# Attention and two mixers on one core: places in a hand-written order of steps, and which PSUM bank a sum reads first

## The chip, the cores and the metric

One core of a Trainium2 chip runs the whole program. The metric is the device time of one execution in microseconds (us), here the median of several runs. TensorE (PE) multiplies, VectorE (DVE) and ScalarE (ACT) do elementwise work, GpSimd (POOL) a few integer additions, SyncE (SP) only issues DMAs.

## What is computed

The input `q`, `k`, `v` goes through an attention (a pooled one over every fourth position and a local one over neighbours), and its output `x` through two mixers. The part of the program that the change touches is the channel part of the first mixer:

```python
h = np.maximum(xt @ w_tok1, 0.0) @ w_tok2
u = x + h.transpose(0, 2, 1)
h2 = np.maximum(u @ w_ch1, 0.0) @ w_ch2
return (u + h2).astype(np.float32)
```

Here `u` is 2304 x 512 (four batches of 576 positions), `w_ch1` 512 x 1536 and `w_ch2` 1536 x 512. The second mixer follows; it multiplies by `w_theta` first, takes sine and cosine, multiplies by two position matrices (`y`), and ends with `u + relu(u @ w_ch)`.

## The kernel before

**Precision.** Every float32 factor is split into a high part and a residual, and a product is three matmuls: high x high, high x residual, residual x high (helper `mm3`, lines 144 to 146). A relu is therefore two instructions: ScalarE writes the high part `h1` (line 862), VectorE then the residual `h2` from the same PSUM bank (line 865).

**Tiling of the channel part.** The 2304 positions are six blocks of 384 (`MIX`). The 1536 hidden channels are twelve slices of 128, numbered `cb` 0 to 11; slices 4 to 11 are done in a second pass, the one that matters here. For one block, this pass is

- the load, the cast and the residual of u (steps `B`, first three), then the first multiplication, one slice after the other (`mix`, lines 638 to 645; 12 matmuls to a slice),
- the relu of each slice (`M block.cb`, `mix_hidden`, line 859: its first step is ScalarE's, its second VectorE's),
- the second multiplication in four groups, one for each 128 output columns (`mix`, lines 647 to 659). A group has 24 matmuls: for slices 4 to 9 twelve that read `h1` (lines 654, 655) and six that read `h2` (line 657), then four that read `h1` of slices 10 and 11 and two that read their `h2`,
- the sum with what the first pass left (`N block.db`, `mix_out`, line 871: an addition and a transpose on VectorE, then DMAs).

Blocks 0 and 1 are done together as a **pair**, with a scheme of seven products instead of eight (Strassen's kind): `PP0.m.i` is product i of slice m (m = 0 to 3) on TensorE (`pair_product`, six matmuls), `PH0.m.i` what is done with its bank (`pair_hidden`). The scheme needs sums of weight quarters, made beforehand (`S0` to `S63`, `weight_parts`, line 664: additions on VectorE and casts on ScalarE), and sums of the two blocks' u (`PT`), and splits of u (`PS`). Products 1 and 2 share a bank `a`, 6, 7 and 4 share `b`; product 5 has `c` and product 3 has `d`. For one hidden slice block 1 needs product 3 + product 6 + v, where v = product 5 + product 1.

**Weights that arrive late.** `X24` to `X40` convert parts of `w_theta`, `w_ri` and `w_ch` (`converted`, line 153). The steps of one part: a DMA, two ScalarE activations, three VectorE operations (lines 183, 185, 193), one GpSimd addition (line 197), a ScalarE cast (line 199), a VectorE residual (line 201). `X39` and `X40` are the last two of `w_ch`. Their staging buffer is released by `R2`; what takes its place are the split parts of x (`ZS`, `cxh` and `cxl`), which the first matmuls of the second mixer (`th`) read. `J5` reloads what block 4 has written out, into the tile `ut` that `N5` adds to.

**What sets the order.** Every step is a Python generator. The string `ORDER` names which generator is advanced next; engines run their instructions strictly in that order, each its own queue:

```python
with tc.manual_schedule(engines={act.engine, dve.engine, pool.engine, pe.engine, nc.sync.engine}):
    for e in ORDER:
        name, _, times = e.partition("*")
        for _ in range(int(times or 1)):
            next(gens[name], None)
```

So a step that stands early in the string and waits holds up everything of its engine that stands behind it. PSUM has eight banks, taken in turn from two pools of four; a bank is taken again once its last reader is through. What comes behind the list (`stage_z`, `stage_y`, `stage_out`, line 1081 on, all of the second mixer) has no such string; the framework's planner orders it.

Of the kernel before, what the change touches and what calls it, by code (L numbers as in the profile page):

```python
# [51 lines left out]
X12 B2 C5 O4.0 X12 X11 X13 C5 O4.3 H5.0 X20 X16 O4.3 X23 B2 C5 H5.1 X10 H5.0 X10 C5 H5.2 X12 X11 X10 H5.1 B2 H5.3 X14  # L52
X10 H5.3 J2 H5.2 X16 C5 M2.4 X23 X10 X16 X23 X15 C5 X18 C5 O5.1 X23 X22 B2 O5.2 O5.0 X12 X15 X14 C5 X23 X14 X16 M2.5
B2 O5.3 X14 X16 O5.3 R1 X18 X15 X23 M2.4 M2.5 X22 X18 X14 B2 X15 X22 X18 M2.6 B2 X18 X14 X22 M2.7 X15 X18 X22 B2 M2.6
M2.8 X22 M2.7 B2 M2.8 M2.9 S0 M2.9 S1 S2 B2 S3 M2.10 S4 M2.10 S8 S5 S6 S9 S7 B3 M2.11 S10 S11 M2.11 S12 S13 S14 S15
S16 S17 B2 S18 S19 S20 S21 B2 S22 N2.0 B3 S23 S24 S25 S26 S27 S28 B3 S29 B2 N2.1 S30 S31 S32 S33 S34 S35 S36 S37 S40
S38 S41 S39 B2 N2.2 S42 S43 S44 S45 S46 N2.0 S47 S48 N2.0 S49 S50 S51 S52 N2.1 B3 S53 N2.3 N2.1 S54 S55 S56 S57 B3
M3.4 S58 S59 S60 M3.4 S61 S62 S63 B3 M3.5 N2.2 R3 PL0 M3.5 PL0 N2.3 PL0 N2.2 B3 M3.6*2 N2.3 B3 M3.7*2 N2.3 B3 M3.8*2
PT0.0 B3 M3.9 PT0.0 M3.9 PT0.0 B3 M3.10 PT0.1 J3 M3.10 PT0.1 M3.11 PT0.1 PS0 M3.11 PT0.3 PS0 PT0.3 B3*2 N3.0 PS0 PT0.3
N3.0 PT0.2 N3.0 PS0 PT0.2 B3 N3.1 PT0.2 N3.1*2 B3 N3.2*3 PP0.0.1 N3.3*2 PP0.1.1 PH0.0.1 N3.3 PP0.0.3 PH0.1.1 PP0.1.3  # L60
N3.3 PP0.0.2 PP0.1.2 PH0.0.2*2 PP0.0.5 PH0.1.2 PP0.1.5 PH0.0.5 J0 PP0.0.6 PP0.1.6 PH0.0.6 PH0.1.5 PP0.2.1 PH0.0.6
PH0.1.6 PH0.0.6 PH0.1.6 PH0.0.6 PH0.1.6 PH0.1.2 PH0.1.6 PP0.3.1 PP0.0.7 PP0.1.7 PH0.0.7*2 PP0.0.4 PH0.1.7 PH0.0.7
PH0.1.7 PP0.1.4 PH0.0.4 PH0.1.7 PH0.0.4 PP0.2.3 PH0.1.4 PH0.0.4 PP0.3.3 PH0.2.1 PH0.3.1 PP0.2.2 PH0.1.4*2 PP0.3.2
PH0.2.2*2 PP0.2.5 PH0.3.2 PP0.3.5 PH0.2.5 PP0.2.6 PP0.3.6 PH0.2.6 PH0.3.5 PP0.2.7 PH0.2.6 PH0.3.6 PH0.2.6 PH0.3.6
PP0.3.7 PH0.2.7 PH0.3.6 PH0.3.7 PH0.2.7 PP0.2.4 PH0.2.6 PH0.3.7 PH0.3.6 PP0.3.4 PH0.2.7 J1 PH0.3.7 B4 PH0.3.2 PH0.2.4
PH0.3.4 PH0.2.4 PH0.3.4 PH0.2.4 PH0.3.4 D1 R5 X28 D1 X29 N1.0 X30 X31 N1.0*2 B4 D1 N1.1 B4 X28*2 X29 D1 N1.2 X28 X30
X29 X32 X28 X30 X29 X33 X29 N1.3 X30 X28 X29 X31 X34 N1.1 D0 N1.2 N1.1 X30 X31 D0 X32 N1.2 N0.0 X31 X30 X32 X33 X35 D0
X31 N0.1 X32 N0.0 N0.1 N0.0 X31 X32 X33 X34 X36 D0 N0.1 N0.2 X33 X32 N0.2 X35 X34 N0.2 X33 B4 N0.3 X34 X33 B4 N0.3
M4.4 X34 X35 N0.3 X36 B4 N0.3 M4.4 X35 M4.5 X34 M4.5 B4 M4.6 X36 X35 B4 M4.7 M4.6 X36 M4.7 J4 X35 X36 B4 N1.3 M4.8
N1.3 X36 M4.8 B4 M4.9 N1.3 M4.9 B4 M4.10*2 B5 M4.11*2 R6 X24 X25 X26 Z B4*2 N4.0*2 B5 N4.0 B5 X24 B4 X24 X25 N4.1 X26  # L70
X24 X25 X27 X24 X26 B4 X25 X37 X25 N4.2 X26 X24 X25 X38 X26 N4.1 B5 N4.3 N4.1 X26 B5 M5.4*2 N4.2*2 B5 M5.5 X27 M5.5 B5
X27 X37 M5.6 X37 X38 X27 B5 X39 X27 M5.6 X37 M5.7 B5 X27 M5.8 X38 X40 X37 B5 M5.9 X37 X38 M5.7 M5.8 X38 B5 M5.9 X39
X38 N4.3 M5.10 X39 N4.3 M5.11 X40 M5.10 N4.3 X39 X40 X39*2 X40 M5.11 B5 X40*2 B5 J5 R2 ZS*4 B5 ZS N5.0 N5.1 N5.0 N5.1
N5.0 ZS*2 B5 N5.2 N5.1 ZS N5.2*2 N5.3*4
""".split()

FINAL = 5
# [28 lines left out]
def kernel(  # L106
# [676 lines left out]
    def pair_hidden(n, m, i):  # L783

        t, key = two[n], place[i]
        ps = t[m, key]
        P, Q = PAIRS[n]

        def tile_of(e, block, cb):
            pool_ = hp if block == P else cells["hx"]  # L790
            return pool_.tile([128, MIX], F32R, tag=f"h{e}", name=f"g{e}_p{block}_{cb}")

        def add(out, x, y):
            dve.tensor_tensor(out=out, in0=x, in1=y, op=ALU.add)

        def finish(block, cb, src):
            h1, h2 = tile_of(1, block, cb), tile_of(2, block, cb)
            act.activation(h1, src, AF.Relu)
            yield
            dve.scalar_tensor_tensor(  # L800
                out=h2, in0=src, scalar=0.0, in1=h1.bitcast(F32), op0=ALU.max, op1=ALU.subtract
            )
            mixes[block, LOWER, "h", 2 * LOWER + cb] = h1, h2
            yield

        if i == 1:
            if m % 2 == 0:
                t["p"] = cells["z"].tile([128, 2, MIX], F32, tag="z", name=f"p_p{n}_{m}")
            t[m, "p"] = t["p"][:, m % 2]
            act.copy(t[m, "p"], ps)  # L810
            yield
        elif i == 2:
            yield from finish(P, m, ps)
        elif i == 5:
            if m % 2 == 0:
                t["vq"] = cells["utx"].tile([128, 4, MIX], F32, tag="ut", name=f"v_p{n}_{m}")
            t[m, "v"], t[m, "q"] = t["vq"][:, m % 2], t["vq"][:, 2 + m % 2]
            add(t[m, "v"], ps, t[m, "p"])
            yield
        elif i == 6:  # L820
            q = t[m, "q"]
            add(q, ps, t[m, "v"])
            yield
            add(q, t[m, "d"], q)
            yield
            yield from finish(Q, m, q)
        elif i == 7:
            add(t[m, "c"], ps, t[m, "v"])
            yield
            yield from finish(Q, 4 + m, t[m, "c"])  # L830
        else:
            add(ps, ps, t[m, "p"])
            yield
            yield from finish(P, 4 + m, ps)
# [198 lines left out]
    for n, pair in enumerate(PAIRS):  # L1033
        step(f"PL{n}", pair_load(n))
        step(f"PS{n}", lazily(lambda n=n: pair_split(n)))
        for k in range(4):
            step(f"PT{n}.{k}", lazily(lambda n=n, k=k: pair_sum(n, k)))
        for m in range(4):
            for i in range(1, 8):
                step(f"PP{n}.{m}.{i}", pair_product(n, m, i))  # L1040
                step(f"PH{n}.{m}.{i}", pair_hidden(n, m, i))
        for i in pair:
            step(f"D{i}", pair_out(i))
# [309 lines left out]
```

## Time and profile before

| what | us |
|---|---|
| median of three runs | 695.96 (692.79 to 696.51) |
| the profiled execution | 695.53 |
| its span, first to last instruction | 693.6 |
| TensorE busy in it | 663.8 |
| VectorE busy | 508.7 |
| ScalarE busy | 317.4 |
| GpSimd busy | 91.8 |

The mean granted TensorE clock of the span is 0.985 of full speed (full speed is 2.4 GHz; the other level is 1.2 GHz, shown as 0.50). Times in the rows are microseconds from the first instruction of the span. The attention ends near 190 us; block 2's second pass has its relus between 278 and 297, the pair its products between 345 and 376, block 5 its relus between 451 and 465, and the second mixer begins at 479.

### The profile page before, as it was taken

To read this page: it belongs to the slowest core of one execution; us is meant where nothing else is said; L and a number is where in the kernel's file an instruction comes from. 1 tells how busy PE (TensorE), PEld (TensorE's weight loads), DVE (VectorE), ACT (ScalarE), POOL (GpSimd) and SP (SyncE) were. 2 spreads that over 40 slices of the span, in tenths; PEclk is the share of its full clock that TensorE was granted. 3 is DMA by queue.
4 is the path that set the end of the run, shared out by engine and by line. 5 is a ranking of instruction groups with operands and counts; after the bars stand their busy time and mean duration, and the time that the engine had idled before them with its cause. 6 is when DMAs were issued, how large, how long until landed. Compare 5 with 4: busy or idle time off the path is not lost.

```text
span 693.6 us, 17324 instructions
## 1 busy us (share of the span) xinstructions
PE 663.8 (96%) x7344; PEld 634.1 (91%) x7344; DVE 508.7 (73%) x916; ACT 317.4 (46%) x618; POOL 91.8 (13%) x79
## 2 busy tenths in 40 slices
PE   7769989999999999989999999989999999999997
PEld 4658869999999999989999999989998998998997
DVE  6979988764543788996645896984887947867836
ACT  4556757443442565443222552552736425526311
POOL 3324222201000432300000231230000000000000
PEclk9979999999999999999999999999999999999999
DMA  8797776554234676207232768954030330140102
GB/s 286 246 277 224 260 240 234 182 168 155 100 131 156 211 260 212 92 7 203 54 104 97 244 129 252 315 151 100 9 129 0 105 116 1 52 146 1 67 3 69
DMA packets 85629, 100.36 MB, mean 145 GB/s; under 512 B 44272, under 2 KB 65904, under 8 KB 85552
## 3 DMA queue, kind: packets, MB, share of 16 engines
q1 hardware_dynamic: 85552, 99.27, 45.5%
q8 instruction: 57, 0.93, 0.5%
q14 instruction: 20, 0.16, 0.1%
HBM read 74.34 MB, written 24.90 MB: 143 GB/s over the span
## 4 chain that ended last, share of the span: by engine, by line
PE 78%; DVE 10%; DMA 7%; ACT 2%; SPq 1%; issue 1%; POOL 0%; DVEq 0%; POOLq 0%
PE y L144 6%; PE y L145 6%; PE y L146 6%; PE c L654 5%; PE c L655 5%; PE c L657 5%; PE c L145 4%; PE c L144 4%; PE c L146 4%; PE th L144 2%; PE th L145 2%; PE th L146 2%; DMA qk<-qkT 2%; PE t L144 2%; PE t L146 2%; PE t L145 2%
## 5 line engine op out<-in xcount | busy, mean ns | idle before, releaser
L197 POOL TENSOR_TENSOR ww<-ww,raw 128x512 int32<-128x512 int32 (+2 forms) x43 | 60.5, 1411 | 291.9 <-PE c_p L849 98.7
L144 PE MATMUL y<-wrh,zh 128*128 128x288 f32 x256 | 75.0, 296 | 0.0
L145 PE MATMUL y<-wrl,zh 128*128 128x288 f32 x256 | 74.9, 296 | 0.0
L146 PE MATMUL y<-wrh,zl 128*128 128x288 f32 x256 | 72.8, 295 | 0.0
L144 PEld LDWEIGHTS y<-wrh,zh 128*128 128x128 f32 x256 | 48.0, 188 | 0.0
L145 PEld LDWEIGHTS y<-wrl,zh 128*128 128x128 f32 x256 | 48.0, 188 | 0.0
L146 PEld LDWEIGHTS y<-wrh,zl 128*128 128x128 f32 x256 | 47.2, 188 | 0.0
L865 DVE SCALAR_TENSOR_TENSOR g<-c,g 128x384 fp32r<-128x384 f32 x56 | 30.0, 550 | 21.3 <-ACT g L862 21.2
L862 ACT ACTIVATE g<-c 128x384 fp32r<-128x384 f32 x56 | 26.7, 491 | 36.8 <-PE c L146 36.5
L180 ACT ACTIVATE ww<-raw 128x512 f32<-128x512 f32 (+2 forms) x43 | 29.2, 679 | 30.4 <-DVE c1l L201 9.5
L144 PE MATMUL c<-uh,c1h 128*128 128x384 f32 x128 | 42.8, 334 | 0.0
L146 PE MATMUL c<-uh,c1l 128*128 128x384 f32 x128 | 42.8, 334 | 0.0
L145 PE MATMUL c<-ul,c1h 128*128 128x384 f32 x128 | 42.8, 334 | 0.0
L873 DVE TENSOR_TENSOR ut<-c,ut 128x384 f32<-128x384 f32 x40 | 21.5, 552 | 25.3 <-PE c L657 23.8
L1133 DVE TENSOR_TENSOR cx<-y,cx 128x288 f32<-128x288 f32 x32 | 14.6, 456 | 32.0 <-PE y L146 31.6
L193 DVE SCALAR_TENSOR_TENSOR ww<-raw,ww 128x512 uint32<-128x512 uint32 (+2 forms) x43 | 31.4, 730 | 1.5
L139 ACT CAST cuh<-cx 128x288 fp32r<-128x288 f32 (+1 forms) x16 | 8.9, 553 | 50.2 <-DVE cx L1133 50.2
L181 ACT ACTIVATE raw<-raw 128x512 int32<-128x512 uint32 (+3 forms) x48 | 31.8, 662 | 0.0
L144 PE MATMUL th<-thh,cxh 128*128 128x512 f32 (+1 forms) x92 | 31.6, 343 | 0.0
L145 PE MATMUL th<-thl,cxh 128*128 128x512 f32 (+1 forms) x92 | 31.6, 343 | 0.0
L146 PE MATMUL th<-thh,cxl 128*128 128x512 f32 (+1 forms) x92 | 31.2, 343 | 0.0
L183 DVE TENSOR_SCALAR ww<-ww 128x512 f32<-128x512 f32 (+2 forms) x43 | 22.9, 534 | 4.6 <-ACT ww L180 4.4
(361 smaller groups left out, 2120.4 us busy)
## 6 DMA issues: line engine op xcount, KB each, us to landing
raw<-w_ch SPq DMA_DIRECT2D x28, 512.0 KB
qk<-qkT SPq DMA_DIRECT2D x16, 582.0 KB
xT<-ut SPq DMA_DIRECT2D x12, 768.0 KB
vd<-vtok SPq DMA_DIRECT2D x8, 650.0 KB
raw<-w_ri SPq DMA_DIRECT2D x9, 576.0 KB
vw<-vloc SPq DMA_DIRECT2D x32, 146.2 KB
uT<-us SPq DMA_DIRECT2D x16, 288.0 KB
ut<-uT SPq DMA_DIRECT2D x6, 768.0 KB
```

Of the source, the lines that this page charges most:

```text
L144: pe.matmul(out, lh, rh, start=start, stop=False, skip_group_check=again)
L145: pe.matmul(out, lh, rl, start=False, stop=False, skip_group_check=again)
L146: pe.matmul(out, ll, rh, start=False, stop=stop, skip_group_check=again)
L180: act.activation(w, high, AF.Abs)
L181: act.activation(f, words[:, :, 0], AF.Copy, scale=2.0**-29)
L193: dve.scalar_tensor_tensor(out=wu, in0=words[:, :, 1], scalar=0xC0000000, in1=wu, op0=ALU.bitwise_and, op1=ALU.bitwise_or)
L197: pool.tensor_tensor(out=w.bitcast(I32), in0=w.bitcast(I32), in1=f, op=ALU.add)
L654: pe.matmul(ps[:, 0:MIX], h[:, cb % 2, d], h1, start=cb == cbs[0], stop=False)
L655: pe.matmul(ps[:, 0:MIX], l[:, cb % 2, d], h1, start=False, stop=False)
L657: pe.matmul(ps[:, 0:MIX], weight[cb // 2][2][:, cb % 2, d], h2, start=False, stop=cb == cbs[-1])
L862: act.activation(h1, ps, AF.Relu)
L865: dve.scalar_tensor_tensor(out=h2, in0=ps, scalar=0.0, in1=h1.bitcast(F32), op0=ALU.max, op1=ALU.subtract)
```

## The change

It changes places in the string at three spots, and in the pair the order of two additions. Before and after, cut to the steps concerned (`*2` is two steps in a row):

```
block 2, before: M2.8 M2.9 S0 M2.9 S1 S2 B2 S3 M2.10 S4 M2.10 S8 S5 S6 S9 S7 B3 M2.11 S10 S11 M2.11 S12
block 2, after:  M2.8 M2.9*2 B2 M2.10*2 M2.11*2 S0 S1 S2 S3 S4 S8 S5 S6 S9 S7 B3 S10 S11 S12

pair, before: PP0.1.5 PH0.0.5 J0 PP0.0.6 PP0.1.6 PH0.0.6 PH0.1.5 PP0.2.1 PH0.0.6
              PH0.1.6 PH0.0.6 PH0.1.6 PH0.0.6 PH0.1.6 PH0.1.2 PH0.1.6 PP0.3.1
pair, after:  PP0.1.5 PH0.0.5*2 J0 PP0.0.6 PP0.1.6 PH0.1.5*2 PH0.0.6 PH0.1.2 PP0.2.1 PH0.1.6
              PH0.0.6*2 PH0.1.6*2 PP0.3.1

block 5, before: M5.9 X39 X38 N4.3 M5.10 X39 N4.3 M5.11 X40 M5.10 N4.3 X39 X40 X39*2 X40 M5.11 B5 X40*2
block 5, after:  M5.9 X39 X38 N4.3 M5.10 M5.11 M5.10 M5.11 X39 N4.3 X40 N4.3 X39 X40 X39*2 X40 B5 X40*2
```

Slices 2 and 3 of the pair get the same new order as slices 0 and 1 (there `PH0.3.2`, which stood at the end of the pair, comes ahead of `PP0.2.7`). Between `X39` and `X40` above stand the same steps as before; nothing is added or left out. In `pair_hidden`:

```diff
             add(t[m, "v"], ps, t[m, "p"])
             yield
+            add(t[m, "q"], t[m, "d"], t[m, "v"])
+            yield
         elif i == 6:
             q = t[m, "q"]
-            add(q, ps, t[m, "v"])
-            yield
-            add(q, t[m, "d"], q)
+            add(q, ps, q)
             yield
             yield from finish(Q, m, q)
```

The number of instructions on every engine stays the same, and so do their shapes.

## Rows read from the trace of the kernel before

**Rows 1.** The page's first part: busy us, share of the span, instructions.

```profile
PE 663.8 (96%) x7344; PEld 634.1 (91%) x7344; DVE 508.7 (73%) x916; ACT 317.4 (46%) x618; POOL 91.8 (13%) x79
```

**Rows 2.** TensorE's waits: line, engine waited for, total us, times, longest.

```profile
PE c L657 <- DVE g L865: 2.2, 2, 2.0
PE c L654 <- ACT g L862: 2.1, 1, 2.1
```

**Rows 3.** Timeline, TensorE, block 2: start us, us, what; first matmuls of four groups.

```profile
290.89 0.33 PE L654 MATMUL c<-g,c22h 128*128 128x384 f32 x1
...
297.88 0.34 PE L654 MATMUL c<-g,c22h 128*128 128x384 f32 x1
...
303.61 0.33 PE L654 MATMUL c<-g,c22h 128*128 128x384 f32 x1
...
307.77 0.33 PE L654 MATMUL c<-g,c22h 128*128 128x384 f32 x1
```

**Rows 4.** Windows: us, busy of PE, PEld, DVE, ACT, POOL, granted clock, DMA share, GB/s.

```profile
299.00:300.00 1.00, 1.00 (x4) 1.00 (x4) 0.87 (x4) 0.53 (x2) 0.00 (x0) 0.50 0.00 0
357.00:358.00 1.00, 0.55 (x3) 0.56 (x4) 1.00 (x3) 0.53 (x1) 0.00 (x0) 1.00 0.03 8
467.00:468.00 1.00, 1.00 (x5) 1.00 (x4) 0.24 (x1) 0.99 (x2) 0.00 (x0) 0.50 0.92 335
```

**Rows 5.** Timeline, TensorE, block 5: first matmuls of the first three groups.

```profile
458.84 0.33 PE L654 MATMUL c<-g,c22h 128*128 128x384 f32 x1
...
465.25 0.33 PE L654 MATMUL c<-g,c22h 128*128 128x384 f32 x1
...
470.99 0.33 PE L654 MATMUL c<-g,c22h 128*128 128x384 f32 x1
```

**Rows 6.** Timeline, ScalarE and VectorE, block 2: relus, residuals, first cast of sums.

```profile
290.20 1.25 ACT L862 ACTIVATE g<-c 128x384 fp32r<-128x384 f32 x3
...
291.78 1.01 DVE L865 SCALAR_TENSOR_TENSOR g<-c,g 128x384 fp32r<-128x384 f32 x2
...
294.96 0.41 ACT L705 CAST s0h<-x 128x256 fp32r<-128x256 f32 x1 [3.51 <-DVE x L672]
...
296.07 0.48 ACT L862 ACTIVATE g<-c 128x384 fp32r<-128x384 f32 x1
```

**Rows 7.** Timeline, TensorE and VectorE, pair: around slice 3's product 1.

```profile
356.57 0.34 PE L146 MATMUL p_a<-uh_p,c1l 128*128 128x384 f32 x1
...
356.83 0.56 DVE L794 TENSOR_TENSOR v_p<-p_d,v_p 128x384 f32<-128x384 f32 x1
...
357.45 0.44 PE L144 MATMUL p_a<-uh_p,c1h 128*128 128x384 f32 x1 [0.54 <-DVE v_p L794]
```

**Rows 8.** Timeline, ScalarE and VectorE, block 5: relus and residuals of slices 10, 11.

```profile
459.18 0.83 ACT L862 ACTIVATE g<-c 128x384 fp32r<-128x384 f32 x2
...
460.76 0.55 DVE L865 SCALAR_TENSOR_TENSOR g<-c,g 128x384 fp32r<-128x384 f32 x1
...
464.36 0.55 DVE L865 SCALAR_TENSOR_TENSOR g<-c,g 128x384 fp32r<-128x384 f32 x1
```

**Rows 9.** Timeline, VectorE and TensorE, from block 5 to the second mixer.

```profile
470.76 1.02 DVE L873 TENSOR_TENSOR ut<-c,ut 128x384 f32<-128x384 f32 x2 [1.44 <-DMA ut<-xT]
...
475.82 0.82 DVE L1001 TENSOR_TENSOR cxl<-cx,cxh 128x640 fp32r<-128x640 f32 x1
...
479.31 0.28 PE L144 MATMUL th<-thh,cxh 128*128 128x256 f32 x1
```

**Rows 10.** Timeline, the pair's loads and first sums beside block 3.

```profile
316.46 0.41 SPq L726 DMA_DIRECT2D tl_p<-uT  x1
...
323.59 0.95 DVE L744 TENSOR_TENSOR z_p<-tl_p,u_p 128x768 f32<-128x768 f32 x1
...
325.06 0.83 ACT L746 CAST th_p<-z_p 128x768 fp32r<-128x768 f32 x1
...
328.57 0.33 PE L654 MATMUL c<-g,c22h 128*128 128x384 f32 x1
```

More of the change, by code (lines that the diff above doesn't have):

```diff
@@ L54 @@
 B2 O5.3 X14 X16 O5.3 R1 X18 X15 X23 M2.4 M2.5 X22 X18 X14 B2 X15 X22 X18 M2.6 B2 X18 X14 X22 M2.7 X15 X18 X22 B2 M2.6
[L55 to L73, printed above, removed]
@@ L74 @@
-N5.0 ZS*2 B5 N5.2 N5.1 ZS N5.2*2 N5.3*4
+M2.8 X22 M2.7 B2 M2.8 M2.9*2 B2 M2.10*2 M2.11*2 S0 S1 S2 S3 S4 S8 S5 S6 S9 S7 B3 S10 S11 S12 S13 S14 S15 S16 S17 B2
+S18 S19 S20 S21 B2 S22 N2.0 B3 S23 S24 S25 S26 S27 S28 B3 S29 B2 N2.1 S30 S31 S32 S33 S34 S35 S36 S37 S40 S38 S41 S39
+B2 N2.2 S42 S43 S44 S45 S46 N2.0 S47 S48 N2.0 S49 S50 S51 S52 N2.1 B3 S53 N2.3 N2.1 S54 S55 S56 S57 B3 M3.4 S58 S59
+S60 M3.4 S61 S62 S63 B3 M3.5 N2.2 R3 PL0 M3.5 PL0 N2.3 PL0 N2.2 B3 M3.6*2 N2.3 B3 M3.7*2 N2.3 B3 M3.8*2 PT0.0 B3 M3.9
@@ new lines @@
+PT0.0 M3.9 PT0.0 B3 M3.10 PT0.1 J3 M3.10 PT0.1 M3.11 PT0.1 PS0 M3.11 PT0.3 PS0 PT0.3 B3*2 N3.0 PS0 PT0.3 N3.0 PT0.2
+N3.0 PS0 PT0.2 B3 N3.1 PT0.2 N3.1*2 B3 N3.2*3 PP0.0.1 N3.3*2 PP0.1.1 PH0.0.1 N3.3 PP0.0.3 PH0.1.1 PP0.1.3 N3.3 PP0.0.2
+PP0.1.2 PH0.0.2*2 PP0.0.5 PH0.1.2 PP0.1.5 PH0.0.5*2 J0 PP0.0.6 PP0.1.6 PH0.1.5*2 PH0.0.6 PH0.1.2 PP0.2.1 PH0.1.6
+PH0.0.6*2 PH0.1.6*2 PP0.3.1 PP0.0.7 PP0.1.7 PH0.0.7*2 PP0.0.4 PH0.1.7 PH0.0.7 PH0.1.7 PP0.1.4 PH0.0.4 PH0.1.7 PH0.0.4
+PP0.2.3 PH0.1.4 PH0.0.4 PP0.3.3 PH0.2.1 PH0.3.1 PP0.2.2 PH0.1.4*2 PP0.3.2 PH0.2.2*2 PP0.2.5 PH0.3.2 PP0.3.5 PH0.2.5*2
@@ new lines @@
+PP0.2.6 PP0.3.6 PH0.3.5*2 PH0.2.6 PH0.3.2 PP0.2.7 PH0.3.6 PH0.2.6 PP0.3.7 PH0.2.7 PH0.3.6 PH0.3.7 PH0.2.7 PP0.2.4
+PH0.2.6 PH0.3.7 PH0.3.6 PP0.3.4 PH0.2.7 J1 PH0.3.7 B4 PH0.2.4 PH0.3.4 PH0.2.4 PH0.3.4 PH0.2.4 PH0.3.4 D1 R5 X28 D1 X29
+N1.0 X30 X31 N1.0*2 B4 D1 N1.1 B4 X28*2 X29 D1 N1.2 X28 X30 X29 X32 X28 X30 X29 X33 X29 N1.3 X30 X28 X29 X31 X34 N1.1
+D0 N1.2 N1.1 X30 X31 D0 X32 N1.2 N0.0 X31 X30 X32 X33 X35 D0 X31 N0.1 X32 N0.0 N0.1 N0.0 X31 X32 X33 X34 X36 D0 N0.1
+N0.2 X33 X32 N0.2 X35 X34 N0.2 X33 B4 N0.3 X34 X33 B4 N0.3 M4.4 X34 X35 N0.3 X36 B4 N0.3 M4.4 X35 M4.5 X34 M4.5 B4
@@ new lines @@
+M4.6 X36 X35 B4 M4.7 M4.6 X36 M4.7 J4 X35 X36 B4 N1.3 M4.8 N1.3 X36 M4.8 B4 M4.9 N1.3 M4.9 B4 M4.10*2 B5 M4.11*2 R6
+X24 X25 X26 Z B4*2 N4.0*2 B5 N4.0 B5 X24 B4 X24 X25 N4.1 X26 X24 X25 X27 X24 X26 B4 X25 X37 X25 N4.2 X26 X24 X25 X38
+X26 N4.1 B5 N4.3 N4.1 X26 B5 M5.4*2 N4.2*2 B5 M5.5 X27 M5.5 B5 X27 X37 M5.6 X37 X38 X27 B5 X39 X27 M5.6 X37 M5.7 B5
+X27 M5.8 X38 X40 X37 B5 M5.9 X37 X38 M5.7 M5.8 X38 B5 M5.9 X39 X38 N4.3 M5.10 M5.11 M5.10 M5.11 X39 N4.3 X40 N4.3 X39
+X40 X39*2 X40 B5 X40*2 B5 J5 R2 ZS*4 B5 ZS N5.0 N5.1 N5.0 N5.1 N5.0 ZS*2 B5 N5.2 N5.1 ZS N5.2*2 N5.3*4
```

## The prediction

> **What bounds the kernel now.** I read the page's busy times first, then TensorE's waits, then the timelines around the three longest waits behind the attention, then what lies downstream of each. TensorE is busy 96% of the span [rows 1], so only what TensorE does not do, or does slowly, can be won. The waits view lists, in the stages that the change touches, 2.1 us of block 2's second multiplication for a relu of ScalarE, and 2.2 us for residuals on VectorE, of which 2.0 lie in block 5 and 0.2 in block 2 [rows 2]. The timeline adds one in the pair: product 1 of slice 3 waits 0.54 us for a sum [rows 7].
>
> A wait costs more than its length. In block 2 the four groups of 24 matmuls should start 4.16 us apart, as the third and fourth do (303.61 to 307.77) [rows 3]. The first takes 290.89 to 297.88, 6.99 us, and the second, which waits for nothing, 5.73 us. The excess is 2.83 + 1.57 = **4.40 us**: 2.3 of waiting, some 0.5 of restarts, and 1.57 because the granted clock was 0.50 (1.2 GHz) between 299 and 300 us [rows 4]. Block 5 repeats it: 458.84 to 465.25 and to 470.99 [rows 5] are 6.41 and 5.74 us, so 2.25 + 1.58 = **3.83 us**, again with a clock of 0.50 [rows 4]. After the pair's short gap the clock stayed at 1.00 [rows 4].
>
> **The change, part by part.** *Block 2.* Today ScalarE has finished three relus of channel slices 8 to 10 at 291.45, then idles 3.51 us until VectorE has made the first weight sums, converts two of them, and only then comes to the relu of slice 11, 296.07 [rows 6]. TensorE ended slice 11 at 291.05 (0.33 us after its last start, one matmul before 290.89). So the relu is five us late only by its place in ScalarE's queue. In the new order it follows slice 10's directly: 291.45 to about 291.95. TensorE wants it at 290.89 + 20 x 0.173 = 294.36. VectorE does its residuals of slices 7 and 8 from 291.78, some 0.47 us each [rows 6]; 9, 10 and 11 now follow without a sum between, done at about 294.2. The last is wanted 23 matmuls after 290.89, at 294.88. Both waits go, with 0.7 us to spare on the tighter, and with the gap the slow stretch: 4.40 us.
>
> Nothing is added. Three residuals, 1.4 us in all, move ahead of the weight sums, so those start 1.4 us later but end when they did, as VectorE has the same work; no queue of DMAs is passed, since the steps moved issue none, and the matmuls of slice 11 (12 of them) pass no other matmul.
>
> *Pair.* The same four additions per slice remain; only which operand comes first changes. Today the addition that reads product 3's bank also needs product 6, so that of slice 1 starts at 356.83; TensorE stops from 356.57 to 357.45 for that bank [rows 7]. In the new order it needs product 5 alone, and can run after the first sum of slice 1, two additions ahead of product 6's. Between slice 1's product 5 and the stop TensorE does three products of 6 x 0.173 = 1.04 us, so product 5 ended near 353.7; one addition of 0.55 us for the first sum and one for the reader of the bank give 354.8, two us before TensorE wants it (356.75). The start-to-start of 0.88 falls to 0.17: **0.7 us**. The chain behind product 6 is one addition (0.55 us) shorter before the relu; TensorE does not wait for that relu, so I count nothing. The earlier addition adds no wait of its own, because product 3 ends before product 5 in TensorE's order; behind it in VectorE's queue stands product 6's reader, which it delays by 0.55 us at most. So a slice pair gains or loses at most 0.55 us there; I take nothing, and leave it to the spread.
>
> *Block 5.* ScalarE does the relus of slices 10 and 11 by 460.0 already; VectorE's residuals follow at 460.76 and 464.36, behind two conversions of a weight part [rows 8]. In the new order both come directly after the relus, done by about 460.7, and wanted at 462.65 and 462.82 (22 and 23 matmuls after 458.84). Two us to spare, so all 3.83 us return. What pays: the conversions start some 1.3 us later (two residuals of 0.47 and a wait for the first relu of 0.4), and through them GpSimd's additions, the cast, the last `wcl`, and the split of x that must wait for that buffer. Behind that split VectorE idles 1.44 us for the reload of `ut` [rows 9], which covers the 1.3. If that cover were gone, 1.3 us would fall on the split, not yet on TensorE (next paragraph). SyncE's queue is passed too (five DMAs of block 4), but it waits for transposes made earlier; I count nothing.
>
> **Do the gains last?** Behind block 2, TensorE runs 4.4 us ahead of loads that do not move: the pair's u and q. VectorE first reads them at 323.59 [rows 10], without a recorded wait, so they had landed by then; SyncE issued the last of them at 316.46; in the new order it comes to that step at about 319.2 and will wait. Behind it stand three residuals of block 3 and on ScalarE three relus. From the read to slice 11's relu I add four VectorE or ScalarE steps of the pair's sums as long as the first (0.95, 0.83, 0.95, 0.95), a second cast of 0.83 and the relu's 0.48 [rows 6, 10]: 5.0 us. TensorE wants it 20 matmuls after 328.57 - 4.40, at 327.64. So a landing up to 322.6 is free; the latest that the trace allows, 323.59, costs 1.0 us there and 0.4 more at the residual. Between 0 and 1.4 I take 0: the free bound leaves the last load 6.1 us from its issue, and 323.59 is only when its reader's turn came. From the pair on, loads and conversions are released by products and so move along with TensorE.
>
> Ahead of the first `th` matmul (479.31) the last split of x ended at 476.64 [rows 9], behind a sum that waits for TensorE. TensorE arrives 3.83 us sooner relative to the loads, at 475.48, and needs that split 11 matmuls of 0.12 us later, 476.8; the split, freed from TensorE, follows the reload (470.76) by about 4 us, 474.7. Two us to spare.
>
> **Sum.** 4.40 + 0.7 + 3.83 = 8.9. The profiled execution took 695.53 us (span 693.6 and 1.9 around it), 0.43 below the median of the runs, 695.96. So 686.6 for such an execution, and **687.0 us** for the median.
>
> Row and rule differ at one point. Both two-us gaps are followed by a clock of 0.50, within three us of the restart, and the short gap is not [rows 4]. The Trainium skill, "TensorE: Matmul & The Clock Gate", section "Why this matters for your kernels", warns of a loss of throughput only for idle gaps longer than these two. By that rule the slow stretches would not belong to the gaps and the sum would be 8.9 - 3.15 = 5.8; the trace speaks against it twice.
>
> **Rivals.**
> *Block 3 gives some back.* The loads land late and TensorE waits 1.4 us in block 3: 688.4, and 690.0 if the clock falls for as long as in block 2. For: the step is in VectorE's queue ahead of residuals that are wanted. Against: the 5 us chain fits with any landing before 322.6.
> *The inputs of `th` do not follow.* If reloads and conversions from 430 to 470 us kept their old times while TensorE comes 8.9 us sooner (470.4), it would wait until 474.7 with 1.3 us of matmuls done in between: 3.0 lost, and 1.6 of slow clock: 691.6. For: VectorE is nearly full there. Against: their start hangs on products of the pair.
> *The slow clock stays.* If it comes from something other than the gaps, 3.15 us do not return: 690.1.
> *The tail is arranged otherwise.* The output stage behind the list is ordered by the framework's own planner, which starts from other times. A lost overlap there, with TensorE waiting on the sine chain and its clock falling, costs what block 2 cost, 4.4 us. One leaves 691.4; three (13.2 us) turn the sum, 700.2, **slower** than before; from 12.4 us lost it decides so. Against: the stage's text is unchanged, and the waits view lists no wait of TensorE in it now.
> *The waits only change their name.* Another semaphore of the same residuals ends just as late: 696.0. Against: each of the three has its input on hand 0.7 to 5 us before it is wanted.
>
> **How the numbers follow.** All three return 0.66; block 3 gives back 0.10; `th` waits 0.07; the clock stays 0.05; a tail with one lost overlap 0.05, with three 0.03; no change 0.04. About 0.5%, 3.5 us, is what a measurement can tell from no change: faster means below 692.5, slower above 699.4. Faster is 0.88 and the greater part of the single lost overlap, 0.91; same 0.06; slower 0.03. Range: downwards half the distance from the median to the lowest run of before (3.2 us) and 0.6 for pauses too short for the waits view, 684.8; upwards through block 3 and the clock with 1 us of spread, 691.0.
>
> **What would show it.** Right: no wait of over 0.3 us on L654, L657 or the pair's `p_a`; groups of block 2 and 5 all 4.16 us apart, granted clock 1.00 throughout; `th` starting some 9 us sooner. Wrong: a new wait in block 3's second multiplication or before `th`; a clock of 0.50 without a gap; output-stage matmuls in another order. A time above 691 would mean that one of the 4-us terms was not there.

## The result, and the profile after

The changed kernel's median is 684.39 us (682.84 to 686.86, six runs) against 695.32 (690.03 to 696.51, six runs) of the kernel before on the same chip: ratio 0.9856, 95% interval 0.9819 to 0.9893. In a second comparison (e11 below) it was 687.94 (681.97 to 690.56) against 694.16 (688.23 to 699.60): ratio 0.9898, interval 0.9845 to 0.9951. (The recorded ratios are estimates over the fast runs and differ a little from the ratios of the medians, 0.984 and 0.991.) Both intervals lie below 1: the change makes the kernel faster, by 0.5 to 1.8%. The forecast was 687.0, with a range of 684.8 to 691.0; the first median lies 0.4 us below that range, the second inside it.

The page's first part for the profiled execution of the kernel after (682.84 us), which answers to [rows 1]:

```profile
span 680.9 us, 17322 instructions
...
PE 659.3 (97%) x7344; PEld 630.2 (93%) x7344; DVE 508.5 (75%) x916; ACT 317.2 (47%) x618; POOL 91.8 (13%) x79
```

The work of VectorE and ScalarE is the same within 0.2 us; TensorE's busy time is 4.5 us shorter; 3.15 us of that are the two slow stretches of [rows 4], in which each matmul counted as busy for longer. The waits of the kernel after, TensorE, as in [rows 2] (line, engine waited for, total us, times, longest):

```profile
PE o L523 <- DVE pbuf L501: 4.0, 1, 4.0
PE o L523 <- issue: 2.0, 1, 2.0
PE sd L389 <- DVE qkd L377: 1.6, 1, 1.6
```

The entries of [rows 2] are gone. All that is listed now has a line of the attention, none of the mixers. The timeline of TensorE in the kernel after, from block 2 to the second mixer, answers to [rows 3], [rows 5], [rows 7] and the last row of [rows 9]:

```profile
287.23 0.33 PE L654 MATMUL c<-g,c22h 128*128 128x384 f32 x1
...
291.39 0.33 PE L654 MATMUL c<-g,c22h 128*128 128x384 f32 x1
...
295.55 0.33 PE L654 MATMUL c<-g,c22h 128*128 128x384 f32 x1
...
299.71 0.33 PE L654 MATMUL c<-g,c22h 128*128 128x384 f32 x1
...
324.32 0.72 PE L657 MATMUL c<-g,c25h 128*128 128x384 f32 x2
324.88 0.33 PE L654 MATMUL c<-g,c22h 128*128 128x384 f32 x1
...
348.75 0.33 PE L146 MATMUL p_a<-uh_p,c1l 128*128 128x384 f32 x1
348.92 0.33 PE L144 MATMUL p_a<-uh_p,c1h 128*128 128x384 f32 x1
...
449.98 0.33 PE L654 MATMUL c<-g,c22h 128*128 128x384 f32 x1
...
454.14 0.33 PE L654 MATMUL c<-g,c22h 128*128 128x384 f32 x1
...
458.30 0.33 PE L654 MATMUL c<-g,c22h 128*128 128x384 f32 x1
...
466.62 0.28 PE L144 MATMUL th<-thh,cxh 128*128 128x256 f32 x1
```

The groups of block 2 and block 5 are 4.16 us apart, and the pair's product 1 of slice 3 (348.92) starts 0.17 us after the matmul ahead of it, the last of slice 2's product 1. One new pause shows, though no list of waits has it: at 324.32, in block 3, two matmuls take 0.72 us where two of this kind take 0.51 in the other groups. The clock where [rows 4] had 0.50 (windows: us, busy of PE, PEld, DVE, ACT, POOL, granted clock, DMA share, GB/s):

```profile
290.00:300.00 10.00, 10.00 (x59) 10.00 (x59) 9.72 (x26) 4.36 (x9) 0.00 (x0) 1.00 0.11 43
...
452.00:462.00 10.00, 10.00 (x60) 10.00 (x59) 7.22 (x12) 4.19 (x7) 2.83 (x2) 1.00 0.57 173
462.00:468.00 6.00, 6.00 (x40) 6.00 (x39) 4.85 (x9) 0.00 (x0) 0.00 (x0) 1.00 0.44 68
```

What the other engines do there, timeline of ScalarE and VectorE of the kernel after, in answer to [rows 6], [rows 8], [rows 9] and [rows 10]:

```profile
286.54 1.63 ACT L862 ACTIVATE g<-c 128x384 fp32r<-128x384 f32 x4
...
288.13 2.40 DVE L865 SCALAR_TENSOR_TENSOR g<-c,g 128x384 fp32r<-128x384 f32 x5
290.46 1.42 DVE L672 TENSOR_TENSOR x<-c1h,c1l 128x256 f32<-128x256 f32 x4
...
318.41 0.96 DVE L744 TENSOR_TENSOR z_p<-tl_p,u_p 128x768 f32<-128x768 f32 x1 [2.80 <-DMA tl_p<-uT]
...
324.00 0.55 DVE L865 SCALAR_TENSOR_TENSOR g<-c,g 128x384 fp32r<-128x384 f32 x1
...
346.56 0.56 DVE L794 TENSOR_TENSOR v_p<-p_d,v_p 128x384 f32<-128x384 f32 x1
...
450.86 1.02 DVE L865 SCALAR_TENSOR_TENSOR g<-c,g 128x384 fp32r<-128x384 f32 x2 [0.34 <-ACT g L862]
...
461.36 1.01 DVE L873 TENSOR_TENSOR ut<-c,ut 128x384 f32<-128x384 f32 x2
...
464.41 0.81 DVE L1001 TENSOR_TENSOR cxl<-cx,cxh 128x640 fp32r<-128x640 f32 x1
```

Four relus and five residuals run in one piece ahead of the weight sums; the two residuals of block 5 end at 451.88; and VectorE now waits 2.80 us for the pair's load, until 318.41.

**Where the difference lies.** The two profiled spans differ by 12.7 us, more than the 8.9 forecast. I cut each span in three: up to block 2's first `L654` matmul, from there to the first `th` matmul, and the rest. The middle stretch took 479.31 - 290.89 = 188.42 us before and 466.62 - 287.23 = 179.39 after: **9.03 us**. The rest took 214.29 and 214.28. The other 3.66 us lie ahead of block 2, where the string, and with it each engine's order, is the same in both kernels.

They can be placed. In the kernel after the same instruction of VectorE starts 0.33 us later than in before near 90 us, and 3.62 us earlier near 122. In between ScalarE casts the input of the mixer's first block, which waits for a load; first before, then after:

```profile
100.72 1.47 ACT L634 CAST uh<-ut 128x1536 fp32r<-128x1536 f32 x1 [5.00 <-DMA ut<-uT]
```

```profile
98.49 1.47 ACT L634 CAST uh<-ut 128x1536 fp32r<-128x1536 f32 x1 [2.43 <-DMA ut<-uT]
```

In before TensorE's first products of that block wait 1.19 and 0.56 us, and the granted clock is 0.50 from 104 to 107 us; in the kernel after neither is there, and the clock is 1.00. The second matmul of that block starts at 104.04 before and at 101.82 after, 2.22 us apart; the rest, 1.4 us, fits the slow clock. So in these two profiles a load that landed about 2 us later, and the slow clock behind it, make the 3.66; nothing in the change touches them.

The table below has all thirteen profiles; the middle column is the measure of the change, since it repeats where the totals scatter.

| kernel | block 2 begins | block 2 to `th` | `th` to the end |
|---|---|---|---|
| before | 290.89 | 188.42 | 214.29 |
| after | 287.23 | 179.39 | 214.28 |
| e11, after once more | 292.14 | 179.44 | 214.42 |
| e1, block 2 alone | 289.80 | 184.92 | 214.28 |
| e2, block 5 alone | 292.83 | 184.60 | 214.27 |
| e3, pair alone | 288.37 | 187.65 | 214.28 |
| e4, pair's additions without new places | 291.84 | 188.28 | 214.28 |
| e5, after, residuals back | 289.59 | 183.54 | 214.27 |
| e6, after, a stop of 0.9 us | 291.40 | 180.29 | 215.11 |
| e7, after, a stop of 1.5 us | 291.21 | 180.98 | 214.31 |
| e8, after, block 3 mended | 288.98 | 179.14 | 214.28 |
| e9, e8 and an attention step | 295.02 | 179.15 | 215.03 |
| e10, e8 and that step placed later | 293.74 | 179.15 | 214.31 |

### The profile page after: what moved, and what is told of

The parts are those of the page before. It is cut to its first block, busy times and chain, and to the rows that moved or that the text cites. A ratio compares the mean times of both kernels' runs of the same rounds, so it can differ in the third digit from the quotient of the medians.

```text
span 680.9 us, 17322 instructions
## 1 busy us (share of the span) xinstructions
PE 659.3 (97%) x7344; PEld 630.2 (93%) x7344; DVE 508.5 (75%) x916; ACT 317.2 (47%) x618; POOL 91.8 (13%) x79
## 4 chain that ended last, share of the span: by engine, by line
PE 89%; DVE 4%; DMA 4%; ACT 1%; SPq 1%; issue 0%; POOL 0%; DVEq 0%; ACTq 0%; POOLq 0%
PE c L654 6%; PE c L144 6%; PE c L657 6%; PE c L655 6%; PE c L145 6%; PE c L146 6%; PE y L144 6%; PE y L145 6%; PE y L146 6%; PE th L144 2%; PE th L146 2%; PE th L145 2%; PE t L144 2%; PE t L146 2%; PE t L145 2%; PE c_p L849 2%
## 5 line engine op out<-in xcount | busy, mean ns | idle before, releaser
L185 DVE TENSOR_SCALAR ww<-ww 128x512 uint32<-128x512 uint32 (+2 forms) x43 | 25.0, 581 | 1.5
```

## The experiments

**e1 to e3: one part of the change at a time.** Each is the kernel before with one of the three edits as the change has it, for e1:

```diff
-M2.8 M2.9 S0 M2.9 S1 S2 B2 S3 M2.10 S4 M2.10 S8 S5 S6 S9 S7 B3 M2.11 S10 S11 M2.11 S12
+M2.8 M2.9*2 B2 M2.10*2 M2.11*2 S0 S1 S2 S3 S4 S8 S5 S6 S9 S7 B3 S10 S11 S12
```

> The kernel before with block 2's new order alone. I read the stretch from block 2's first L654 matmul to the first th matmul (188.42 us before, 179.39 with the whole change). My theory, gap and slow clock both belong to the late relu: the two waits in block 2 go, its four groups start 4.16 us apart, the granted clock there is 1.00, and the stretch shortens by 4.40 us, to 184.0; total about 691. Rival, the slow clock has another cause and stays: 2.83 come back, 185.6, and a clock of 0.50 still shows near 299 us. Rival, block 3 gives some back, since its loads don't move: a new wait of TensorE in block 3's second multiplication, 185.4 or more. Block 5 and the pair keep their waits in all three.

Measured for e1: ratio 0.9973 (0.9942 to 1.0004), which holds 1 and shows nothing by itself; stretch 184.92, 3.50 us shorter. The four groups of block 2 are 4.15, 4.17 and 4.15 us apart, so the 4.40 came back whole, slow clock and all. Of it 0.73 was lost again in block 3, whose first two groups took 4.87 and 4.18 us instead of 4.16 (the rest, 0.17, is block 5's own stop, longer than in the profile of before). TensorE's timeline of e1 in block 3, and its clock after block 2's first group and after block 5's stop:

```profile
327.66 0.44 PE L657 MATMUL c<-g,c25h 128*128 128x384 f32 x1 [0.28 <-DVE g L865]
```

```profile
292.00:300.00 8.00, 8.00 (x48) 8.00 (x47) 7.72 (x23) 3.10 (x7) 0.00 (x0) 1.00 0.21 78
...
462.00:464.00 2.00, 2.00 (x8) 2.00 (x7) 1.21 (x3) 1.61 (x3) 0.00 (x0) 0.50 0.98 337
```

So my theory held for block 2, and the rival "block 3 gives some back" held too: the two are about different stages. Where block 5's stop stayed, its clock of 0.50 stayed.

> The kernel before with block 5's new order alone. The same stretch. My theory: the 2.0 us wait goes with its slow clock, 3.83 us, 184.6; TensorE reaches th without a wait. Rival, the slow clock stays: 2.25 come back, 186.2. Rival, the split of x comes too late because the conversions are pushed back: a wait before th of up to 1.3 us, 185.9. Total about 692 by the first.

Measured for e2: ratio 0.9928 (0.9896 to 0.9960), stretch 184.60, shorter by 3.82. No wait ahead of `th`. Both rivals fall.

> The kernel before with the pair's change alone (the two additions exchanged and the new places). My theory: product 1 of slice 3 starts 0.17 us after the matmul ahead of it instead of 0.88, so the stretch is 0.7 us shorter, 187.7; the small pause near 372 us of before, some 0.15 us, may go too, 187.6. Rival, another reader of the same banks ends as late: 188.4. If the three parts add up to the whole change (9.03), e1, e2 and this give 4.4 + 3.8 + 0.7 to 0.9. A total within the scatter of before in either case.

Measured for e3: ratio 1.0005 (0.9977 to 1.0032), which tells nothing of 0.8 us in 695. In the trace, from the pair's first product to block 4's first `L654` matmul, TensorE takes 79.31 us instead of 80.35: **1.04**, and the same 79.31 stands in the kernel after. (The stretch as a whole shrank by only 0.77, since block 5's stop happened to be 0.4 us longer and block 2's slow clock 0.1 us shorter than before.)

The parts make 4.40 + 3.82 + 1.04 = 9.26; the whole is 9.03, and block 3's groups in the kernel after (4.37 and 4.19 instead of 4.16) account for the 0.24 between.

**e4: what of the pair's edit does the work.** The additions are exchanged in the code, but stay in the slots of VectorE's queue that the kernel before has:

```diff
-PH0.0.6 PH0.1.5 PP0.2.1 PH0.0.6 PH0.1.6 PH0.0.6 PH0.1.6 PH0.0.6
+PH0.0.5 PH0.1.5 PP0.2.1 PH0.0.6 PH0.1.5 PH0.0.6 PH0.1.6 PH0.0.6
-PP0.3.6 PH0.2.6 PH0.3.5 PP0.2.7 PH0.2.6 PH0.3.6 PH0.2.6
+PP0.3.6 PH0.2.5 PH0.3.5 PP0.2.7 PH0.2.6 PH0.3.5 PH0.2.6
```

> The kernel before with only the two additions of the pair exchanged, each left in the slot of VectorE's queue that an addition of that slice had before; none of the new places. It tells which half of the pair's change does the work. My theory: what held bank d was the operand (product 6), not the slot; slice 1's reader of the bank now stands fourth or fifth in the run of additions that begins at 354.85 in the trace of before, and ends by 356.3, ahead of the 356.75 at which TensorE wants it, so the wait of 0.54 is gone and the stretch is 187.7 as in the pair's whole change. Rival, the place is what counts: the reader still ends after 357 and the wait of some 0.5 us stays, 188.4.

(In slice 2 this kernel's addition reads bank `b` only after product 7 has been added to it, so that slice's sums are others.) Ratio 0.9995 (0.9958 to 1.0031). The timeline of VectorE and TensorE in e4:

```profile
356.27 0.55 DVE L794 TENSOR_TENSOR v_p<-p_d,v_p 128x384 f32<-128x384 f32 x1
...
372.61 0.56 DVE L794 TENSOR_TENSOR v_p<-p_b,v_p 128x384 f32<-128x384 f32 x1 [2.62 <-PE p_b L146]
...
374.27 0.44 PE L144 MATMUL p_b<-th_p,s3h 128*128 128x384 f32 x1 [1.71 <-DVE v_p L794]
```

For slices 0 and 1 the theory holds: slice 1's reader of the bank runs at 356.27, and product 1 of slice 3 follows without a stop. So there the exchange alone was enough. In slices 2 and 3 the old slots are too late for another reason: products 6 and 7 share bank `b`, the reader of product 6 now stands behind product 7, and TensorE stops for 1.71 us. The pair took 81.27 us, 0.92 more than before. The stretch, 188.28, is near the rival's 188.4 by luck: 0.92 was lost here, and 1.06 won where block 5's stop was for once not followed by the slow clock (last section). The exchange needs the new places; neither half of the edit is idle.

**e5: half of block 2's edit.** The kernel after, with the relu left early and the residuals put back among the weight sums:

```diff
-M2.8 M2.9*2 B2 M2.10*2 M2.11*2 S0 S1 S2 S3 S4 S8 S5 S6 S9 S7 B3 S10 S11 S12
+M2.8 M2.9 S0 M2.9 S1 S2 B2 S3 M2.10 M2.11 S4 M2.10 S8 S5 S6 S9 S7 B3 S10 S11 M2.11 S12
```

> The changed kernel with half of block 2's change undone: the relu of slice 11 stays early in ScalarE's queue, the residuals of slices 9 to 11 go back among VectorE's weight sums (slice 11's stands behind ten sums of about 0.335 us). It asks whether the wait of before belonged to the relu, which the waits view names, or to the place of the whole pair of steps. My theory: the residual then ends 10 x 0.335 = 3.35 us after its end in the changed kernel (290.5), 293.85, and TensorE wants it at 291.2, so the wait only changes its name: some 2.6 us on VectorE's residual, and with the slow clock behind it the stretch from block 2's first L654 matmul to the first th matmul grows from 179.39 to 183.5 (182.0 if the clock stays up). Rival, the relu alone was late: 179.4.

(e5, e6 and e7 were executed once each; what is said of them rests on one profile.) Stretch 183.54, as the theory has it. TensorE's waits (line, engine, total us, times, longest), its timeline and its clock in e5:

```profile
PE c L657 <- DVE g L865: 2.3, 2, 1.7
```

```profile
294.14 0.44 PE L657 MATMUL c<-g,c25h 128*128 128x384 f32 x1 [0.57 <-DVE g L865]
296.29 0.45 PE L657 MATMUL c<-g,c25h 128*128 128x384 f32 x1 [1.70 <-DVE g L865]
```

```profile
297.00:300.00 3.00, 3.00 (x11) 3.00 (x10) 2.83 (x8) 2.17 (x5) 0.00 (x0) 0.50 0.00 0
```

The first two groups take 6.98 and 5.73 us, as long as before (6.99 and 5.73), though the relu that [rows 2] names is early. In before the list of waits gave nearly all of the stop to ScalarE's relu; the residuals behind it on VectorE would have come as late. Moving ScalarE's step alone is worth nothing in block 2.

**e6 and e7: shorter stops.** The kernel after, with only slice 11's residual behind five or seven sums (e6 shown):

```diff
-M2.11*2 S0 S1 S2 S3 S4 S8
+M2.11 S0 S1 S2 S3 S4 M2.11 S8
```

> The changed kernel with the residual of block 2's slice 11 put behind five weight sums (5 x 0.335 = 1.7 us, of which 0.7 are to spare), so TensorE stops for about 1.0 us. It asks from what length of gap the clock falls. Theory, the slow clock belongs to gaps of two us and more only: the second group stays at 4.16 us and the stretch is 180.4 (179.39 + 1.0 + 0.2 for the restart, less the 0.2 pause in block 3). Rival, any real stop brings it: second group 5.4 to 5.7 us, the stretch 181.9.

> The same with seven weight sums ahead of that residual: TensorE stops for about 1.6 us (7 x 0.335 - 0.7). If the clock falls here and not after the 1.0 us stop, the length decides, and the stretch is 179.39 + 1.6 + 0.2 + 1.5 - 0.2 = 182.5; if it stays up, 181.0. After the pair-only variant of before a 2.5 us stop in block 5 was not followed by a fall, while four others of 2.0 to 2.4 us were, so a third theory is that length alone doesn't decide; a stop of 1.6 us then may go either way.

Stretches 180.29 and 180.98. The recorded waits are 0.87 and 1.54 us, and the clock behind them stayed up (windows of e6, then e7):

```profile
297.00:304.00 7.00, 7.00 (x43) 7.00 (x42) 6.72 (x18) 3.74 (x8) 0.00 (x0) 1.00 0.00 0
```

```profile
297.00:304.00 7.00, 7.00 (x41) 7.00 (x42) 6.73 (x17) 3.61 (x7) 0.00 (x0) 1.00 0.00 0
```

The second groups take 4.17 and 4.18 us. Here a stop of 1.5 us cost itself and 0.3 of restart, no more. (The 2.5 us stop that the expectation of e7 speaks of is e4's; the stops of 2.0 to 2.4 us seen by then were seven, see the last section.)

**e8: block 3 mended.** The kernel after, with three residuals ahead of the sum that waits for a load:

```diff
-M3.8*2 PT0.0 B3 M3.9 PT0.0 M3.9 PT0.0 B3 M3.10 PT0.1 J3 M3.10 PT0.1 M3.11 PT0.1 PS0 M3.11 PT0.3 PS0
+M3.8*2 B3 M3.9*2 PT0.0 B3 M3.10 PT0.0 M3.10 PT0.0 M3.11 PT0.1 J3 M3.11 PT0.1*2 PS0 PT0.3 PS0
```

> The changed kernel with block 3's relus and residuals of slices 9 to 11 moved ahead of the pair's first sums of u (steps PT), which wait for loads that the change didn't move. In the changed kernel block 3's first group of 24 matmuls took 4.37 us instead of 4.16 and the second 4.19 (0.24 us given back), with block 2's change alone 4.87. My theory: residuals no longer stand behind the sum that waits 2.8 us for a load, all four groups are 4.16 us, and the stretch is 179.15. Rival, the sums that are now later hold up the pair's products: the 0.24 come back as a wait on p_a or p_c, 179.4 or more. Totals within the scatter of the changed kernel, 683 to 687, in either case.

Ratio 0.9890 (0.9853 to 0.9926), stretch 179.14, all groups of block 3 at 4.16. VectorE and TensorE of e8 around slice 11's residual (323.95):

```profile
320.22 0.96 DVE L744 TENSOR_TENSOR z_p<-tl_p,u_p 128x768 f32<-128x768 f32 x1 [0.79 <-DMA tl_p<-uT]
...
323.95 0.55 DVE L865 SCALAR_TENSOR_TENSOR g<-c,g 128x384 fp32r<-128x384 f32 x1
...
326.07 0.51 PE L657 MATMUL c<-g,c25h 128*128 128x384 f32 x2
326.42 0.33 PE L654 MATMUL c<-g,c22h 128*128 128x384 f32 x1
```

The residual ends at 324.50, 1.7 us before TensorE wants it (326.24), where in the kernel after it ended 0.05 us late. The pair's products lose nothing by it (79.30 us). The 0.25 us repeats in e9 and e10, which contain this edit; the medians of e8 and of the kernel after cannot be told apart.

**e9 and e10: a step of the attention.** Its longest wait in the kernel after is a bank that VectorE reads late, because two additions ahead of the read wait for a transfer. The kernel of e8, for e10 (e9 moves `L5` alone, ahead of both `L3`):

```diff
-K6 L5 F1 G1 L3 A0 V2 X0 A1 L3 G1 T0 L5 G0
+K6 L5 F1 G1 L3*2 L5 A0 V2 X0 A1 G1 T0 G0
```

> The kernel of e8 (block 3 mended) with one step of the attention moved in the same manner: the maximum and subtraction of the local attention's fifth pair, which read a PSUM bank that TensorE wants back, come ahead of the two additions that wait for a transfer. In the changed kernel VectorE idles 2.61 us there for that transfer and TensorE then waits 4.0 us for the bank, its longest wait. My theory: the wait goes to under 1 us; what follows on TensorE needs the split of x behind those additions, which start up to 1.4 us later, so 1.5 to 2.5 us come back by the first token product (near 47 us), and at most that by block 2's first L654 matmul. Rival, the early part of the attention runs at the pace of its transfers (DMA busy 80% there), and the next transfer ends as late as now: nothing comes back, block 2 begins at 288 to 291 us as in the other runs. The stretch from block 2 to th stays 179.1.

> The kernel of e8 with the attention's step moved once more, now behind the transposes of the buffer that it writes into (in e9 it stood ahead of them, so that those read the next pair's values: a changed part of the computation). First theory: VectorE's reads of the bank no longer stand behind the wait for a transfer, TensorE's longest wait of the attention (2.5 to 4.2 us in the runs so far) falls below 1.5 us, and up to 1.5 us come back by the first token product, which began at 50.3 to 54.7 us (its fifteenth matmul) in ten runs. Rival: e9 shows that wait gone and block 2 no earlier (295.0), because the early attention goes at the pace of its loads, which scatter by more; then block 2 begins at 287 to 293 us again. The stretch from there to th stays 179.1, as in e8.

Measured: e9 0.9898 (0.9848 to 0.9947), block 2 at 295.02; e10 0.9905 (0.9867 to 0.9942), at 293.74. The wait of `o` for the bank is 0.7 us in e10 and not listed in e9, but others take its place (TensorE's first waits in e9):

```profile
PE s L488 <- issue: 8.2, 4, 3.1
PE pdt L432 <- ACT pd L428: 3.9, 2, 2.2
```

Nothing came back: block 2 began later in both than in any of the other profiles. The rival holds as far as the result goes. That the loads set the pace there is not shown: the first of these waits has no releaser in the profile (`issue`), and I tried no kernel that takes a load away.

**e11: the changed kernel once more.**

> The changed kernel once more, beside e10. It asks what of the 12.7 us between the two first profiles belongs to the change. My theory: the stretch from block 2's first L654 matmul to th is 179.1 to 179.4 again, from th to the end 214.3, and the stretch ahead of block 2, which has the same instructions in both kernels, is anywhere from 287 to 293 us as in the runs so far. Rival, the change also shortened what lies ahead of it, through another placement of buffers or transfers: 287 again, and below every run of a kernel without block 2's new order (288.4 to 292.8).

Block 2 began at 292.14, 4.91 us later than in the first profile of the same program; the stretch was 179.44. TensorE's first waits in e11:

```profile
PE pdt L432 <- DVE ods L462: 3.6, 1, 3.6
PE s L485 <- ACT id L303: 3.1, 1, 3.1
PE o L523 <- DVE pbuf L501: 2.0, 1, 2.0
```

Over the eleven profiles that share the attention's code block 2 begins between 287.23 and 292.83. The rival falls: the 3.66 us belong to no kernel. It also shows how much a single profile of this kernel can be off, as a total.

## Why the prediction was right

**Block 2, 4.40 us: right to the hundredth**, in e1 and in the kernel after. The residual of slice 11 ended at 290.53, with 0.7 us to spare as worked out. e5 shows that the relu's move alone is not enough; the residual reads what the relu writes, so its move needs the relu's.

**Block 5, 3.83: right**, 3.82 in e2. The residuals ended at 451.88, wanted at 453.96 (23 matmuls after 449.98): two us to spare. The cover named for the later conversions was used: the 1.44 us that VectorE idled for a reload [rows 9] are gone at 461.36. The last split of x ended at 465.22, 2.7 us before its matmul (466.62 and 11 x 0.12).

**Pair, 0.7: right in its mechanism, mis-sized; it measured 1.04.** Slice 1's reader of the bank ended at 347.12, 1.8 us before TensorE wanted it (348.92); two were forecast. The term took the start-to-start of the stop alone, 0.88 to 0.17. The matmul behind it also started late, by 0.11 (0.28 instead of 0.17), and there was a second pause, 0.2 us in slice 3's product 7: in the profile of before it went on at 372.36, where VectorE's reader of product 6, which holds that bank, ended at 372.31. The step "a slice pair gains or loses at most 0.55 us there; I take nothing" was the wrong one: the second pair of slices had something to gain.

**Block 3, 0: wrong by 0.24.** The step that failed is "a landing up to 322.6 is free". It priced the relu of slice 11: 5.0 us from the read of the load to the relu's end, measured 5.07 (318.41 to 323.48), and TensorE wanted it 0.5 us later, as forecast. But the tighter end was the residual, 0.4 us tighter by the prediction's own next line, and that was left out of the bound. Set back to the times of before, the load was read at 322.07 in the kernel after, 322.12 in e11 and 322.54 in e1. Slice 11's residual then ended 0.05, 0.10 and 0.54 us after TensorE wanted it, and the first group lost 0.21, 0.27 and 0.71 us: the lateness and 0.16 or 0.17 of restart. So by these three the bound lies near 322.0, 0.6 lower than mine. e8 takes the steps apart and the loss is gone.

**The slow clock belongs to the stops: held**, for 3.15 of the sum. In none of the thirteen profiles did the clock fall between block 2 and `th` without a stop of TensorE just ahead. The reverse does not hold: not every such stop was followed by a fall (last section).

**Other rivals.** `th` did not wait. The output stage kept its order and its 214.28 us. "The waits only change their name" is false for the change as made and true for half of it (e5).

**The sum.** Forecast 8.9, measured 9.03 and 8.98 in the stretch; the errors of the pair (+0.34) and of block 3 (-0.24) nearly cancel. That the sum came within 0.1 us is in part luck. 9.0 of 695.3 us is a ratio of 0.987, which lies in both intervals of the totals. The 1.9 us that the first pair of medians shows beyond it are within the interval (7.4 to 12.6 us). The lower end of the range was set too near: it allowed 2.2 us, worked out from three runs of before, while the beginning of block 2 alone scatters by 5.6 us over eleven profiles.

## What to carry to other kernels

Where an order is fixed by hand, look behind every wait for what stands ahead of the awaited instruction in its own engine's queue, and ahead of its companions in theirs: moving only the one that the list of waits names can bring nothing. When a stretch is shortened, check every read of a load that did not move along, at the tightest of its consumers and not the first; put reads that may wait for a transfer behind what TensorE wants soon. And where one part of a program scatters by more than the change is worth, compare the time between two marks that enclose the change alone.

## What was not expected of the hardware

Between block 2 and `th`, a stop of TensorE of some two us was followed by a clock of 0.50 (1.2 GHz) in most runs, not all. Recorded waits and what followed there:

| stop | wait, us | clock behind it |
|---|---|---|
| block 2, in before, e2, e3, e4 | 2.08 to 2.09, then 0.19 | 0.50 each time |
| block 2, e5 | 0.57, then 1.70 | 0.50 |
| block 5, in before, e1, e3 | 1.98, 2.12, 2.39 | 0.50 each time |
| block 5, e4 | 2.47 | 1.00 |
| pair, e4 | 1.71 | 1.00 |
| block 2, e7 and e6 | 1.54, 0.87 | 1.00 |

The odd one is e4: the longest wait of the table, at a place where three shorter ones were followed by a fall. TensorE's timeline of e4 at that stop, and the windows behind its stops in block 2 and block 5:

```profile
467.33 0.44 PE L657 MATMUL c<-g,c25h 128*128 128x384 f32 x1 [2.47 <-DVE g L865]
```

```profile
299.00:301.00 2.00, 2.00 (x8) 2.00 (x8) 1.73 (x6) 1.17 (x4) 0.00 (x0) 0.50 0.00 0
...
468.00:475.00 7.00, 7.00 (x42) 7.00 (x41) 4.49 (x8) 3.23 (x5) 0.00 (x0) 1.00 0.38 115
```

So the length of a stop alone does not decide, and 1.7 us is no bound for safety either. Near 103 us, ahead of the stretch of the table, TensorE of before waited 0.68, 1.19 and 0.56 us within some three us, and the clock fell to 0.50; in e4 it waited 0.37, 2.09 and 0.56 at the same place, and the clock stayed at 1.00. What decides was not settled. The price, where the clock fell in the table, was 1.2 to 1.6 us in the group behind the stop. The Trainium skill, "TensorE: Matmul & The Clock Gate", section "Why this matters for your kernels", warns of idle gaps longer than any stop of the table. Eight stops here with waits of 1.98 to 2.39 us (e5's is split in two) were followed by the lower clock, so to stay below the gaps that the page warns of was not enough for this kernel.
